# One third-feature block per token block moved from a DMA transpose to TensorE, with the first products reordered around the turns

## The chip, the cores and the metric

The kernel runs on one core of a Trainium2 chip. The metric is the time of one execution in device microseconds. TensorE multiplies matrices, VectorE and ScalarE do elementwise work and read TensorE's results out of PSUM, GpSimd (POOL in the profile) does small elementwise work, and SyncE (SP) issues most DMAs. [...]

## The reference

The input `x` has 2048 tokens (L) of 640 features (H), all in bfloat16. Two branches work on the same `x`, and a gate per token mixes them.

```python
    def _A_ref(x, Lambda_re, Lambda_im, B_re, B_im, C_re, C_im, log_dt, Dskip):
        ...
        Lam_bar = jnp.exp(dt * Lam)
        B_bar = ((Lam_bar - 1.0) / Lam)[:, None] * Bmat
        Bu = jnp.einsum("bld,pd->blp", x + 0j, B_bar)
        ...
        for t in range(L):
            h = Lam_bar[None, :] * h + Bu[:, t, :]
            hs.append(h)
        hseq = jnp.stack(hs, 1)
        y = 2.0 * jnp.einsum("blp,dp->bld", hseq, Cmat).real + x * Dskip[None, None, :]
        return y

    def _B_ref(x, w1, b1, w2, b2):
        h = jnp.einsum("bsd,df->bsf", x, w1) + b1
        h = _gelu(h)
        return jnp.einsum("bsf,fd->bsd", h, w2) + b2

    x = A_x
    g = _sigmoid((x * gate_w).sum(-1, keepdims=True))
    ...
    return g * a + (1 - g) * b
```

Branch A is a diagonal complex state-space model with 640 states; branch B is a two-layer perceptron with 1728 hidden units.

## The kernel before

**Tiles and stages.** Tokens are cut into four chunks of 512 (`CH`), each of four blocks of 128 (`TPC` = 4). Where the change speaks of "tokens 0 and 1" it means token blocks 0 and 1 of the first chunk. Features are cut into five blocks of 128 (`KD` = 5), and the hidden units of branch B into 14 blocks (`KF`). TensorE contracts over partitions, so the products need `x` with features on partitions: `xT[c]` holds chunk c as [feature in block, feature block, token]. `xn[c]` holds the same chunk as it lies in memory, tokens on partitions. The program goes through stages that it writes out at its end: `ff1` (first layer of B), `ssm` (input product of A and its scans), `fin_b` (second layer of B) and `fin_a` (output product of A), for the four chunks in an interleaved order.

**The start, where the change lies.** The first products, L361 to L397, compute the first six hidden blocks (`FA` = 6) of chunk 0. They accumulate in six PSUM banks, `banks[0..5]`, over the five feature blocks. Two ways bring chunk 0's features onto partitions:

- Feature blocks 0 and 1 (`KA` = 2) are loaded plainly into `xn[0]` by `load_x0`, one DMA per token block, and turned by TensorE: `turn` (L239) multiplies a 128 x 128 block of `xn[0]` with the identity into a PSUM bank, and `turned` (L243) copies the result into `xT[0]`, on VectorE for feature block 0 and on ScalarE for feature block 1. `turn_first(a, other, t)` does both for token block a.
- Feature blocks 2, 3 and 4 come by two DMA transposes (`load_turned`, L149), one for token blocks 0 and 1, one for 2 and 3. The plain copy of these features for later use in branch A is loaded much later (L186, L187).

All turns write into two PSUM banks, `pA` and `pT`. `pT` takes feature block 0 and `pA` feature block 1, each with 128 columns per token block. `pA` has another use at L391.

**PSUM.** `bank()` (L75) hands out tiles of one pool, `ps`, of eight buffers[...]. At the start `pA`, `pT` and the six `banks` are alive. The next tile, `pP` (L373), is for turning a small array of parameters, `prmA`; its copy into `colA` (L375) starts a chain on VectorE and ScalarE that makes sine and cosine tables for branch A.

**The first products.** `strip(kd, t0, t1, f0, f1)` issues the products of feature block kd with tokens t0 to t1 for hidden blocks f0 to f1, one matmul each, and `part(kd, a)` is a strip over token block a and all six hidden blocks. Weights for feature block kd and the six hidden blocks are in `w1a[kd]`.

**What sets the order.** For TensorE, VectorE and ScalarE the order in the program is the order on the engine (`manual_schedule`, L195). Each engine runs its own instructions in that order and waits where one needs a result of another. DMAs go out from SP's queue and, for three of the first loads, from ScalarE's, in program order as well: x of token blocks 0, 1 and 3 and `w1a[2]` on SP; `w1a[0]`, `w1a[1]` and x of block 2 on ScalarE; then the two transposes, `w1a[4]`, `w1a[3]`, `w1b`, `w1c` and the weights of branch A on SP. GpSimd's queue loads the small parameters. Later in the program a small clock model (`ck`, with `pend` and `let_out`) decides where VectorE's scan work is placed; it is entered with `ff1_mm` through `pe(cols)`, which only adds columns.

Of the kernel before, what the change touches and what calls it, by code (L numbers as in the profile page):

```python
# [16 lines left out]
P = 128  # L17
T = 2048
D = 640
# [3 lines left out]
KD = D // P  # L23
# [5 lines left out]
H = TPC // 2  # L29
HT = H * P  # L30
KSA = 2
HD = D // 2
FA = 6
# [8 lines left out]
def kernel(  # L42
# [19 lines left out]
    nc = tc.nc  # L62
    x2d = A_x.flatten_outer_dims()
# [11 lines left out]
    def bank(dtype=F32):  # L75
        return ps.tile([P, CH * 4 // (4 if dtype == F32 else 2)], dtype, name="bank")
# [6 lines left out]
    xT = [const.tile([P, KD, CH], BF16, name=f"xT{c}") for c in range(NCH)]  # L83
# [41 lines left out]
    def load_w1a(queue, kd):  # L125
        queue.dma_start(out=w1a[kd][:], in_=B_w1[kd * P:(kd + 1) * P, 0:cut1])
# [2 lines left out]
        queue.dma_start(out=dst, in_=v.rearrange("(j p) -> j p", p=P))  # L129

    KA = 2
    xn[0] = xnp.tile([P, TPC, D], BF16, name="xn")

    def load_x0(queue, a0, a1, d0, d1):
        queue.dma_start(out=xn[0][:, a0:a1, d0:d1], in_=x2d[a0 * P:a1 * P, d0:d1].rearrange("(a p) d -> p a d", p=P))

    load_x0(nc.sync, 0, 1, 0, KA * P)
    load_w1a(nc.scalar, 0)
    load_x0(nc.sync, 1, 2, 0, KA * P)
    load_w1a(nc.scalar, 1)  # L140
    load_x0(nc.sync, 3, 4, 0, KA * P)
    load_x0(nc.scalar, 2, 3, 0, KA * P)
    load_w1a(nc.sync, 2)
# [2 lines left out]
    warm = const.tile([P, 1], F32, name="warm")  # L146
    nc.scalar.activation(out=warm[:], in_=nc.const_aps.tensor(1.0, [P, 1], BF16), func=ACT.Exp)

    def load_turned(a):  # L149
        nc.sync.dma_start_transpose(out=xT[0][:, KA:KD, a * P:(a + H) * P], in_=x2d[a * P:(a + H) * P, KA * P:D])  # L150

    load_turned(0)
    load_turned(H)
    load_w1a(nc.sync, 4)
    load_w1a(nc.sync, 3)
    for kd in range(KD):
# [26 lines left out]
        nc.sync.dma_start(out=w2_sb[:, k0:k1, :], in_=B_w2[k0 * P:k1 * P, :].rearrange("(kf p) d -> p kf d", p=P))  # L183
    for h in range(2):
        nc.sync.dma_start(out=w2l[h * F_LAST:(h + 1) * F_LAST, :], in_=B_w2[(KF - 1) * P:F, :])
    load_x0(nc.sync, 0, H, KA * P, D)  # L186
    load_x0(nc.sync, H, TPC, KA * P, D)  # L187
    nc.sync.dma_start(out=b2bc[:], in_=B_b2.rearrange("(o d) -> o d", o=1).to_broadcast([P, D]))
    nc.sync.dma_start(out=Dbc[:], in_=A_Dskip.rearrange("(o d) -> o d", o=1).to_broadcast([P, D]))
# [45 lines left out]
    pA = bank()  # L235
# [3 lines left out]
    def turn(p, col, a, kd):  # L239
        nc.tensor.matmul(p[:, col:col + P], lhsT=xn[0][:, a, kd * P:(kd + 1) * P], rhs=ident[:], start=True, stop=True,  # L240
                         skip_group_check=True)

    def turned(engine, p, col, a, k0, k1):  # L243
        dst = xT[0][:, k0:k1, a * P:(a + 1) * P]
        src = p[:, col:col + (k1 - k0) * P].rearrange("p (k t) -> p k t", t=P)
        if engine is nc.vector:
            nc.vector.tensor_copy(out=dst, in_=src)
        else:
            nc.scalar.activation(out=dst, in_=src, func=ACT.Identity)

    def turn_first(a, other, t=None):
        t = t or bank()
        turn(t, a * P, a, 0)
        turned(nc.vector, t, a * P, a, 0, 1)
        turn(other, a * P, a, 1)
        turned(nc.scalar, other, a * P, a, 1, 2)

    pT = bank()
# [16 lines left out]
    def ff1_mm(p, c, kf, kd, t0=0, t1=CH, first=None, last=KD - 1):  # L275
        w, f0 = (w1a, 0) if kf < FA else (w1b, FA) if kf < FB else (w1c, FB)
        w = w[kd][:, (kf - f0) * P:(kf - f0 + 1) * P]
        nc.tensor.matmul(p[:, t0:t1], lhsT=w, rhs=xT[c][:, kd, t0:t1],  # L278
                         start=(kd == 0) if first is None else first, stop=(kd == last), skip_group_check=first is not None)
        pe(t1 - t0)  # L280
# [53 lines left out]
    def strip(kd, t0, t1, f0=0, f1=FA):  # L334
        for kf in range(f0, f1):
            ff1_mm(banks[kf], 0, kf, kd, t0, t1, kf not in begun, 3)
            begun.add(kf)
# [17 lines left out]
    def over(c, n):  # L355
        return c.rearrange("p (k o) -> p k o", o=1).to_broadcast([P, KS, n])

    def part(kd, a):
        strip(kd, a * P, (a + 1) * P)

    for _ in range(3):  # L361
        nc.tensor.matmul(banks[0][:, 0:P], lhsT=ones(P), rhs=ones(P), start=True, stop=True, skip_group_check=True)  # L362
    turn_first(1, pA, pT)
    part(0, 0)
    part(0, 1)
    strip(1, 0, HT, 0, FA // 2)
    turn_first(3, pA, pT)
    strip(1, 0, HT, FA // 2, FA)
    turn_first(2, pA, pT)
    part(0, 3)  # L370
    part(1, 3)
    part(0, 2)
    pP = bank()  # L373
    nc.tensor.matmul(pP[:, 0:2 * KS], lhsT=prmA[:], rhs=ident[:, 0:2 * KS], start=True, stop=True, skip_group_check=True)  # L374
    nc.vector.tensor_copy(out=colA[:], in_=pP[:, 0:2 * KS])  # L375
# [1 line left out]
    nc.vector.tensor_scalar(out=limp[:], in0=lim_c, scalar1=INV_2PI, scalar2=None, op0=ALU.mult)  # L377
    nc.vector.tensor_tensor(out=thp_c[:], in0=dt16[:], in1=limp[:], op=ALU.mult)
    nc.vector.tensor_tensor(out=u, in0=tf[:].rearrange("p (o i) -> p o i", o=1).to_broadcast([P, KS, NP]), in1=over(thp_c[:], NP), op=ALU.mult)
    part(1, 2)  # L380
    strip(2, 0, HT)
    nc.vector.tensor_copy(out=kk[:], in_=u)
# [48 lines left out]
    for ks in range(KS):  # L431
        for dst, X, xs, Y in ((TCOS, FS, nsH, FC), (TSIN, FC, sH, FS)):
            t = work.tile([P, HB], F32, name="g")
# [305 lines left out]
```

## Time and profile before

| What | Value |
|---|---|
| Median of 8 runs | 215.14 us (214.58 to 216.46) |
| The profiled execution's own time | 215.41 us |
| Its span | 213.5 us |
| TensorE, VectorE, ScalarE, POOL busy | 98%, 86%, 48%, 29% of the span |
| Products of the first layer from `w1a` (L278) | 152 matmuls, mean 340 ns |
| Turns (L240) | 8 matmuls, from 3.36 to 6.90 us |
| Cast out of a turn on VectorE (L247), on ScalarE (L249) | 0.29 us, 0.28 us |

The span runs from the first to the last instruction that the profiler recorded; the execution's own time also holds what lies around it. In the timeline, each line gives a start in us from the span's start, a duration, the engine, the line of the kernel, what is written and read, and how many instructions were merged; what stands in brackets is the idle time before and what ended it. PE is TensorE's multiplication and PEld its loading of the stationary operand. A duration of a matmul includes its latency, so the distance from start to start tells how long it holds TensorE.

### The profile page before, as it was taken

How to read it: one execution, taken by the hardware profiler on the slowest of the kernel's cores; microseconds unless marked ns; L12 is line 12 of the kernel's file. 1: busy time of each engine (PE TensorE's matmuls, PEld its weight loads, DVE VectorE, ACT ScalarE, POOL GpSimd, SP SyncE). 2: the span in 40 equal slices, each digit the busy share in tenths (PEclk: the TensorE clock that was granted, in tenths of full speed). 3: DMA queues.
4: the chain of work that ended last, by engine and by line, in shares of the span. 5: the costliest groups of instructions: out<-in, count | busy, mean ns of one | idle time of the engine just before them, and what ended most of it. 6: DMA issues, size and time to landing. Idle time of an engine off the chain costs nothing.

```text
span 213.5 us, 3580 instructions
## 1 busy us (share of the span) xinstructions
PE 209.3 (98%) x1365; PEld 125.7 (59%) x1376; DVE 183.2 (86%) x335; ACT 102.1 (48%) x184; POOL 62.8 (29%) x101
## 2 busy tenths in 40 slices
PE   8999999999999999999999999999999999999994
PEld 5844444454576644775457777444457587676773
DVE  1589999999998999999999999999999999903153
ACT  3499856665858588203663210456682422305100
POOL 7035069854441563404145503055000000000000
PEclk9999999999999999999999999999999999999999
DMA  6999999997000000061000005100000000100011
GB/s 185 249 179 216 231 232 341 244 185 186 3 0 0 0 3 0 12 186 64 0 0 3 0 1 186 61 0 0 0 3 15 0 3 31 61 31 3 0 63 64
DMA packets 33314, 16.24 MB, mean 76 GB/s; under 512 B 24720, under 2 KB 33296, under 8 KB 33296
## 3 DMA queue, kind: packets, MB, share of 16 engines
q1 hardware_dynamic: 32560, 15.50, 30.2%
q10 hardware_dynamic: 576, 0.49, 0.7%
q8 instruction: 11, 0.18, 0.3%
q14 instruction: 7, 0.06, 0.1%
q0 software_dynamic: 160, 0.01, 0.1%
HBM read 7.48 MB, written 2.62 MB: 47 GB/s over the span
## 4 chain that ended last, share of the span: by engine, by line
PE 98%; issue 0%; DVE 0%
PE bank L606 27%; PE bank L278 27%; PE bank L665 20%; PE bank L549 20%; PE bank L237 1%; PE bank L622 1%; PE bank L300 1%; PE bank L240 0%; DVE ot L670 0%; PE bank L362 0%; PE bank L391 0%; PE bank L374 0%
## 5 line engine op out<-in xcount | busy, mean ns | idle before, releaser
L606 PE MATMUL bank<-w_sb,gel 128*128 128x384 bf16 (+1 forms) x416 | 57.9, 299 | 0.0
L606 PEld LDWEIGHTS <-gel 128*128 128x128 bf16 x416 | 40.3, 98 | 17.0 <-issue 0.8
L552 ACT ACTIVATE bu<-bank 128x512 bf16<-128x512 f32 x40 | 23.6, 606 | 37.5 <-PE bank L549 37.5
L283 ACT ACTIVATE gel<-bank,colB 128x512 bf16<-128x512 f32 x52 | 34.0, 695 | 10.8 <-PE bank L278 10.6
L665 PEld LDWEIGHTS <-hs 128*128 128x128 bf16 x330 | 31.7, 98 | 11.6
L513 POOL TENSOR_SCALAR e<-g,cq 128x2 f32<-128x2 bf16 x15 | 18.3, 1222 | 64.3 <-DVE g L506 64.3
L506 DVE TENSOR_TENSOR_SCAN g<-r_c,carry,v 128x512 bf16<-128x512 f32 x30 | 37.2, 1270 | 0.0
L614 ACT ACTIVATE gb<-bank,gcol 128x384 f32<-128x384 f32 (+1 forms) x32 | 15.1, 526 | 33.7 <-PE bank L622 16.8
L278 PE MATMUL bank<-xT,w1a 128*128 128x512 bf16 (+2 forms) x152 | 27.9, 340 | 0.2
L665 PE MATMUL bank<-CT_re,hs 128*128 128x320 bf16 (+2 forms) x165 | 27.1, 295 | 0.0
L665 PE MATMUL bank<-CT_im,hs 128*128 128x320 bf16 (+2 forms) x165 | 27.1, 295 | 0.0
L670 DVE SCALAR_TENSOR_TENSOR ot<-bank,gcol,gb 128x320 bf16<-128x320 f32 (+2 forms) x33 | 17.4, 532 | 9.7 <-PE bank L665 9.5
L549 PE MATMUL bank<-xT,BT_im 128*128 128x512 bf16 x99 | 24.8, 379 | 0.1
L549 PE MATMUL bank<-xT,BT_re 128*128 128x512 bf16 x97 | 24.4, 379 | 0.2
L278 PEld LDWEIGHTS <-w1a 128*128 128x128 bf16 x156 | 14.4, 103 | 11.7
L580 DVE TENSOR_TENSOR bank<-xn,Dbc 128x320 f32<-128x320 bf16 (+2 forms) x33 | 14.5, 483 | 7.0 <-ACT gb L614 7.0
L278 PE MATMUL bank<-xT,w1b 128*128 128x512 bf16 x80 | 17.9, 379 | 0.0
L549 PEld LDWEIGHTS <-BT_im 128*128 128x128 bf16 x100 | 9.8, 98 | 11.8
L549 PEld LDWEIGHTS <-BT_re 128*128 128x128 bf16 x100 | 9.6, 98 | 11.0
L515 POOL TENSOR_TENSOR carry<-e,e 128x1 f32<-128x1 f32 x30 | 15.8, 547 | 1.2
L487 DVE TENSOR_TENSOR v<-wa,wb 128x512 bf16<-128x512 bf16 x40 | 15.2, 422 | 0.6
L595 ACT ACTIVATE bank<-b2bc 128x384 f32<-128x384 bf16 (+1 forms) x24 | 11.7, 529 | 7.1 <-DVE ot L670 7.1
(110 smaller groups left out, 216.6 us busy)
## 6 DMA issues: line engine op xcount, KB each, us to landing
out_dram<-ot SPq DMA_DIRECT2D x15, 160.0 KB, 1.8
w_sb<-in_B_w_dram SPq DMA_DIRECT2D x2, 640.0 KB, 6.0
xn<-in_A_x_dram SPq DMA_DIRECT2D x2, 640.0 KB, 4.2
w_sb<-in_B_w_dram SPq DMA_DIRECT2D x1, 800.0 KB, 9.6
w1b<-in_B_w_dram SPq DMA_DIRECT2D x5, 128.0 KB, 3.3
xn<-in_A_x_dram SPq DMA_DIRECT2D x4, 160.0 KB, 2.8
w1a<-in_B_w_dram SPq DMA_DIRECT2D x3, 192.0 KB, 3.4
w1a<-in_B_w_dram ACTq DMA_DIRECT2D x2, 192.0 KB, 3.0
```

What stands on the lines that cost most here:

```text
L278: nc.tensor.matmul(p[:, t0:t1], lhsT=w, rhs=xT[c][:, kd, t0:t1], start=(kd == 0) if first is None else first, stop=(kd == last), skip_grou ...
L283: nc.scalar.activation(out=gel[c][:, kf, :], in_=p[:, :], func=ACT.Gelu_apprx_tanh, bias=b1_c[:, kf:kf + 1])
L487: nc.vector.tensor_tensor(out=o, in0=a, in1=b, op=op)
L506: nc.vector.tensor_tensor_scan(s["g"][:, ri, :], r_c[:, ks:ks + 1].to_broadcast([P, CH]), s["v"][:, ri, :], init, ALU.mult, ALU.add)
L513: nc.gpsimd.tensor_scalar(out=t[:], in0=g[:, :, CH - 1], scalar1=f[:, ks:ks + 1], scalar2=None, op0=ALU.mult)
L515: nc.gpsimd.tensor_tensor(out=carry[:, ri, ks:ks + 1], in0=m[0][:, ri:ri + 1], in1=m[1][:, 1 - ri:2 - ri], op=op)
L549: nc.tensor.matmul(p[:], lhsT=BT[ks >= KSA][:, kd, (ks % KSA if ks < KSA else ks - KSA) * P:][:, 0:P], rhs=xT[c][:, kd, :], start=(kd == 0 ...
L552: nc.scalar.activation(out=bu[:, ri, :], in_=p[:], func=ACT.Identity)
L606: nc.tensor.matmul(p[:, col:col + d1 - d0], lhsT=gel[c][:, kf, a * P:(a + 1) * P], rhs=w2_sb[:, kf, d0:d1], start=False, stop=False, skip_ ...
L614: nc.scalar.activation(out=gbs[ti][:, d0:d1], in_=p[:, col:col + d1 - d0], func=ACT.Identity, scale=gcol[:, 1, ti:ti + 1])
L665: nc.tensor.matmul(p[:, 0:d1 - d0], lhsT=hs[c][:, j, lo:lo + P], rhs=CT[:, j % KS, d0:d1], start=False, stop=(j == 2 * KS - 1), skip_group ...
L670: nc.vector.scalar_tensor_tensor(out=ot[:, d0:d1], in0=p[:, 0:d1 - d0], scalar=gcol[:, 0, ti:ti + 1], in1=gbs[ti][:, d0:d1], op0=ALU.mult, ...
```

## The change

Token blocks 0 and 1 now load three feature blocks plainly (`KB` = 3), and the first DMA transpose brings only feature blocks 3 and 4 for them. The second transpose still brings three. The late plain load of the rest of token blocks 0 and 1 becomes one feature block narrower. TensorE makes two more turns, for feature block 2 of token blocks 0 and 1; the first goes into `pT` with its copy on VectorE, the second into `pA` with its copy on ScalarE. They stand ahead of `pP`.

The products of feature blocks 0 and 1 are issued in another order. Three of the six products of token block 0 go ahead of the turn of token block 1. Block 3 is turned earlier, and the products of feature block 1 with token blocks 0 and 1 become two parts of 128 columns in place of two half strips of 256 columns. `part(0, 2)` and `part(1, 2)` stand after `pP`'s matmul and the instructions of VectorE and ScalarE that follow it in the program.

```diff
     KA = 2
+    KB = 3
...
-    load_x0(nc.sync, 0, 1, 0, KA * P)
+    load_x0(nc.sync, 0, 1, 0, KB * P)
     load_w1a(nc.scalar, 0)
-    load_x0(nc.sync, 1, 2, 0, KA * P)
+    load_x0(nc.sync, 1, 2, 0, KB * P)
...
-    def load_turned(a):
-        nc.sync.dma_start_transpose(out=xT[0][:, KA:KD, a * P:(a + H) * P], in_=x2d[a * P:(a + H) * P, KA * P:D])
-
-    load_turned(0)
-    load_turned(H)
+    def load_turned(a, k):
+        nc.sync.dma_start_transpose(out=xT[0][:, k:KD, a * P:(a + H) * P], in_=x2d[a * P:(a + H) * P, k * P:D])
+
+    load_turned(0, KB)
+    load_turned(H, KA)
...
-    load_x0(nc.sync, 0, H, KA * P, D)
+    load_x0(nc.sync, 0, H, KB * P, D)
...
+    strip(0, 0, P, 0, FA // 2)
     turn_first(1, pA, pT)
-    part(0, 0)
+    strip(0, 0, P, FA // 2, FA)
+    part(1, 0)
+    turn_first(3, pA, pT)
     part(0, 1)
-    strip(1, 0, HT, 0, FA // 2)
-    turn_first(3, pA, pT)
-    strip(1, 0, HT, FA // 2, FA)
+    part(1, 1)
+    part(0, 3)
     turn_first(2, pA, pT)
-    part(0, 3)
     part(1, 3)
-    part(0, 2)
+    for a, t, engine in ((0, pT, nc.vector), (1, pA, nc.scalar)):
+        turn(t, a * P, a, KA)
+        turned(engine, t, a * P, a, KA, KB)
     pP = bank()
     nc.tensor.matmul(pP[:, 0:2 * KS], lhsT=prmA[:], rhs=ident[:, 0:2 * KS], start=True, stop=True, skip_group_check=True)
...
+    part(0, 2)
     part(1, 2)
     strip(2, 0, HT)
```

## The prediction

> **What bounds the kernel now.** I read the page first: busy times, then the chain that ended last. TensorE is busy for 98% of the span and the chain is TensorE from end to end.
>
> ```profile
> span 213.5 us, 3580 instructions
> PE 209.3 (98%) x1365; PEld 125.7 (59%) x1376; DVE 183.2 (86%) x335; ACT 102.1 (48%) x184; POOL 62.8 (29%) x101
> ...
> PE 98%; issue 0%; DVE 0%
> ```
>
> The view of waits, cut to TensorE, has one row for the whole execution: the start itself.
>
> ```profile
> PE bank L237 <- PEq L723: 0.8, 1, 0.8
> ```
>
> So nothing that makes data arrive sooner shortens this execution; time is won or lost only by what TensorE must issue, by gaps between its instructions, and by its clock. Busy time cannot show short gaps, because the ends of matmuls are modelled and overlap the next start. The timeline's start times show them. I read it around the turns (L240), which the change multiplies.
>
> ```profile
> 3.68 0.29 DVE L247 CAST xT<-bank 128x128 bf16<-128x128 f32 x1 [2.21 <-PE bank L240]
> ...
> 4.03 0.37 PE L240 MATMUL bank<-ident,xn 128*128 128x128 bf16 x2
> ...
> 6.81 0.31 PE L240 MATMUL bank<-ident,xn 128*128 128x128 bf16 x2
> ...
> 6.95 1.17 PE L278 MATMUL bank<-xT,w1a 128*128 128x128 bf16 x18
> 7.06 0.29 DVE L247 CAST xT<-bank 128x128 bf16<-128x128 f32 x1 [0.31 <-PE bank L240]
> 7.15 0.28 ACT L249 ACTIVATE xT<-bank 128x128 bf16<-128x128 f32 x1 [0.30 <-PE bank L240]
> 7.90 0.10 PEld L374 LDWEIGHTS <-prmA 128*128 128x128 bf16 x1
> 7.96 0.17 PE L374 MATMUL bank<-ident,prmA 128*128 128x10 bf16 x1
> ```
>
> Three readings. (a) Slot: 18 products of 128 columns between 6.95 and 7.96 are 0.056 us each. Before about 6.5 us the starts stand twice as far apart (4.20, 4.30, 4.41, 4.52): 0.107 us. (b) Token block 1's turn starts at 4.03, just after the cast out of block 0's part of the same bank ended (3.68 + 0.29 = 3.97), although it writes other columns. At 6.46 + 0.29 = 6.75 the cast of block 3 ended, and block 2's turn follows at 6.81. So a turn waits for the last copy out of its bank. (c) That round trip, turn to copy to next use of the bank, is 0.25 (6.81 to 7.06) + 0.29 + 0.06 = 0.60 us by VectorE, and 0.25 + 0.28 + 0.05 = 0.58 us by ScalarE.
>
> Of the DMA transposes I read issue and landing:
>
> ```profile
> L150 SPq DMA_TRANSPOSE xT<-in_A_x_dram x2: 1275/1300/1325, 2.6 to 4.0; - x2
> ...
> DMA to landing us min/median/max: 3.8/4.2/4.6
> ```
>
> The first is issued at 2.59 and lands 4.6 later, at 7.2; the second at 3.97 + 3.8 = 7.8. The groups by window put their first users, the products of 256 columns, at 8.3 (blocks 0 and 1) and 9.0 (blocks 2 and 3): 1.1 and 1.2 us of slack.
>
> [...] 0.107 us a slot, then 0.056, with the switch near 6.5 us. [...] The first x load (64 KB, issued on SP) and w1a_0 (192 KB, on ACT), both issued at 0.72, land 2.6 and 2.8 us later[...].
>
> **The change, part by part.**
>
> *Bigger x loads.* Blocks 0 and 1 bring 96 KB each instead of 64; the number of DMA issues on SP and ACT stays. Upper bound: 32 KB at the page's 185 GB/s for the first slice is 0.18 us. Lower: w1a_0 carries 128 KB more than the x load and lands 0.2 us later, so 0.05 for 32 KB. I take 0.1 us later for the first turn (3.36). TensorE is then on the half clock[...]: **+0.05** (0.02 to 0.18). Block 1's load, landing about 0.2 to 0.3 late near 4.0, is covered: its turn now follows the first three products, near 4.45. w1a_0 and w1a_1, up to 0.2 late, are used near 4.13 and 5.0, against landings at 3.5 and 4.3.
>
> *Shorter transpose.* Six blocks of 128 x 128 become four, so SP's issue falls from 1.33 to about 0.88 us and the other transpose, w1a_4, w1a_3, w1b and w1c go out about 0.4 us earlier. TensorE waits for none: **0**.
>
> *Two more turns.* 2 x 0.056 = **+0.11**. One more 0.29 us cast and one 0.28 us activation lie on engines that idle there (0.84 and 0.96 us before L375 and L376).
>
> *The order.* The products are the same in number of columns; six of 256 columns become twelve of 128, equal within 0.02. Three products ahead of block 1's turn need only w1a_0 and block 0's first cast, for which the turn itself waited before: 0. Block 3's turn comes nine products after block 1's: covered. Then two short covers:
>
> 1. Block 2's turn, six products (block 1 of features, token block 3), then block 0's third-feature turn into `pT`. Starts would be 8 slots apart, 0.45 us; the bank needs 0.60: **+0.15**. The turn into `pA` needs 0.58 after block 2's, which has passed by then.
> 2. `pP = bank()` is the ninth tile of a pool of eight. `pA` and six accumulators live on, so it can only take `pT`'s bank. Before, 18 products stood between the last turn and pP's matmul (6.81 to 7.96, against 0.60 needed). Now pP follows the last `pT` turn after one turn: 0.11 against 0.60, **+0.49**. In TensorE's queue behind it stand part(0, 2), part(1, 2) and everything later. They do not need pP, but cannot pass.
>
> The old order has a smaller case, which goes: at 6.81 and 6.90 block 2's turns started together about 0.06 later than the spacing allows: **-0.06**.
>
> Bounds for the two covers: 0.35 if the copies answer 0.15 faster each, 0.9 if a wait costs 0.13 more each. Nothing below zero: an instruction cannot precede the copy it waits for.
>
> *Who waits for pP.* The colA copy on VectorE and the chain behind it, sine tables included. By the sum pP goes from 7.96 to about 8.35, 0.4 later, whereas TensorE's products after it go 0.74 later. GELU and table work therefore gain cover, and no later wait is made. POOL's queue is not touched except for colA's reader at 8.45, which no one awaits soon.
>
> Sum: 0.05 + 0.11 + 0.15 + 0.49 - 0.06 = **+0.74 us**. As TensorE never waits later, nothing gives it back. The profiled execution, 215.41 us, becomes 216.15. It lies 0.27 above the median of 215.14, inside the scatter of 214.58 to 216.46; taken to the median: **215.9 us**, +0.34%, own range 215.5 to 216.4. A measurement of this kernel tells some 0.3%, 0.65 us, from no change.
>
> **Rivals.**
>
> *The bank wait is mostly covered (0.15).* If the copies are back sooner or pP gets another bank, only the start and the turns remain: +0.16, 215.3. Against it: readings (b) and (c), and the count of the banks.
>
> [...]
>
> *The data is what binds elsewhere, and the change is faster (0.15).* Place: the products of feature block 2, L381. With the clock up at 4.2 instead of 6.5 they would start (6.5 - 4.2)/2 = 1.15 earlier, at 7.15, just where the first transpose lands. In executions without the profiler it may land later still; the change takes blocks 0 and 1 off that transpose. Decision point: the wait removed must exceed 0.74, and 1.4 for a gain that can be told, so a landing 1.4 us after the need. That gives 214.4 or less. Against: 1.1 us of slack and no DMA wait on TensorE.
>
> **How the numbers follow.** My forecast holds 0.62, of which 0.08 falls inside 0.65 us since its centre stands near that line. Slower: 0.54 + 0.08[...] = 0.62. Same: 0.08 + 0.15 = 0.23. Faster: 0.15. The range 214.4 to 217.0 takes in the bounds of the covers, the mostly covered rival and the near part of the faster one; about 0.1 is left below and 0.07 above.
>
> **What would show it.** In the timeline after: ten turns; block 0's third-feature turn about 0.60 after block 2's; pP's matmul about 0.60 after that, with TensorE starting nothing between but one turn; the first product of feature block 2 near 9.0 instead of 8.3; the spacing of later products unchanged. Wrong if pP's matmul follows the turn within 0.2 us, if products of L278 wait for a DMA[...].

## The result: slower by a quarter of a per cent, and the profile after

| | Median | Runs |
|---|---|---|
| Before | 214.71 us (214.28 to 216.46) | 58 |
| Changed | 215.22 us (214.86 to 216.06) | 21 |

The ratio is 1.0026 with a 95% interval of 1.0015 to 1.0036: +0.56 us, from 0.32 to 0.77 (the two medians differ by 0.51). The change costs time, as forecast. The centre is below the 0.74 us of the forecast and below the 0.3% that I had called the least that can be told; the interval still reaches to 0.77, so this number by itself does not contradict the size.

The page of the changed kernel still has TensorE as its chain. A cast on VectorE (L248) has entered it.

```profile
span 213.1 us, 3597 instructions
...
PE 208.6 (98%) x1373; PEld 125.1 (59%) x1384; DVE 183.6 (86%) x336; ACT 102.7 (48%) x185; POOL 63.1 (30%) x101
...
PE 98%; DVE 0%; issue 0%
PE bank L611 27%; PE bank L279 26%; PE bank L670 20%; PE bank L554 20%; PE bank L238 1%; PE bank L627 1%; PE bank L301 1%; PE bank L241 0%; DVE xT L248 0%; DVE ot L675 0%; PE bank L378 0%; PE bank L396 0%
```

The span is 0.4 us *shorter* than before, although the kernel is slower: the profiled execution, 214.93 us, had an early clock. Its products are one slot of 0.056 us apart from the first one at 3.97; in the profile of before that spacing began near 6.5, after 0.107 us. By full clock and half rate I mean these two spacings alone: the granted clock reads 1.00 in the profile of before at both, from 4.20 to 6.30 and from 7.00 to 7.90. The 2.5 us between 4.0 and 6.5 at half rate are worth some 1.25 us (an estimate from the two slots: half of them). Two single executions of this kernel can't be compared by their spans.

What can be compared is the distance between starts. The view of waits, cut to TensorE's products and then to its weight loads, has two new rows that name another engine or a DMA:

```profile
PE bank L378 <- DVE xT L248: 0.3, 1, 0.3
```

```profile
PEld L241 <- DMA xn<-in_A_x_dram: 0.2, 1, 0.2
```

And the timeline of the changed kernel around the last turns, with start and duration in front:

```profile
6.07 0.28 PE L241 MATMUL bank<-ident,xn 128*128 128x128 bf16 x2
...
6.18 0.50 PE L279 MATMUL bank<-xT,w1a 128*128 128x128 bf16 x6
6.33 0.29 DVE L248 CAST xT<-bank 128x128 bf16<-128x128 f32 x1 [0.82 <-PE bank L241]
...
6.67 0.27 PE L241 MATMUL bank<-ident,xn 128*128 128x128 bf16 x2
...
6.93 0.29 DVE L248 CAST xT<-bank 128x128 bf16<-128x128 f32 x1 [0.31 <-PE bank L241]
...
7.27 0.17 PE L378 MATMUL bank<-ident,prmA 128*128 128x10 bf16 x1 [0.33 <-DVE xT L248]
```

The six products from 6.18 end their slots at 6.52; the third-feature turn starts at 6.67, 0.60 after block 2's turn at 6.07. That is the hole of 0.15. `pP`'s product starts at 7.27, again 0.60 after the turn, where two turns fill only 0.11: the hole of 0.49. The brackets show 0.33 for it, and the first hole has no bracket at all, since the modelled end of a product covers its first part. Both holes stand where the forecast put them.

### The profile page after: what moved, and what is told of

Read it like the earlier page. It is cut to its first block, busy times and chain, and to the rows that moved or that the text cites. A ratio compares the mean times of both kernels' runs of the same rounds, so it can differ in the third digit from the quotient of the medians.

```text
span 213.1 us, 3597 instructions
## 1 busy us (share of the span) xinstructions
PE 208.6 (98%) x1373; PEld 125.1 (59%) x1384; DVE 183.6 (86%) x336; ACT 102.7 (48%) x185; POOL 63.1 (30%) x101
## 4 chain that ended last, share of the span: by engine, by line
PE 98%; DVE 0%; issue 0%
PE bank L611 27%; PE bank L279 26%; PE bank L670 20%; PE bank L554 20%; PE bank L238 1%; PE bank L627 1%; PE bank L301 1%; PE bank L241 0%; DVE xT L248 0%; DVE ot L675 0%; PE bank L378 0%; PE bank L396 0%
## 5 line engine op out<-in xcount | busy, mean ns | idle before, releaser
L279 PE MATMUL bank<-xT,w1a 128*128 128x512 bf16 (+2 forms) x158 | 27.0, 322 | 0.3
L279 PEld LDWEIGHTS <-w1a 128*128 128x128 bf16 x162 | 13.9, 98 | 12.2 <-issue 0.6
```

## The experiments

Ten kernels gave results, two of them twice. Times without a gate scatter by over 1 us, and in the ungated traces the slot of TensorE falls from 0.107 to 0.056 us (the clock rises, as I call it) at moments from 3.7 to 6.6 us. So most kernels were gated: a wait ahead of the first turn is to make the executions start the real work at one time, at full clock, with the first inputs landed.

```diff
     pA = bank()
-    for n in (512, 512, 512, 512, 512, 128, 128, 128, 128):
-        nc.tensor.matmul(pA[:, 0:n], lhsT=ones(P), rhs=ones(n), start=True, stop=True)
+    gate = work.tile([P, 2, CH], BF16, name="v")
+    nc.vector.memset(gate[:], 0.0)
+    for _ in range(5):
+        nc.scalar.activation(out=gate[:], in_=gate[:], func=ACT.Identity)
+    for _ in range(22):
+        nc.tensor.matmul(pA[:, 0:512], lhsT=ones(P), rhs=ones(512), start=True, stop=True)
+    nc.tensor.matmul(pA[:, 0:512], lhsT=ones(P), rhs=gate[:, 0, :], start=True, stop=True)
```

The first turn then starts at 9.20 in the traces, with slots of 0.056 us in those of g_before_2 and g_after, and most runs of one kernel agree within 0.15 us. Six of the 41 gated executions are 1.2 to 1.6 us longer, with a mean granted clock of 0.992 where the others have 0.998 or more; one of them is the profiled execution of g_before, in which TensorE had waited 1.9 us at the gate (0.9 to 1.7 in the other traces) and ran at half rate from 10.45 to 13.7. The table compares traces of the others.

| Gated kernel | Median, us | Last five output products start at | Against before |
|---|---|---|---|
| before, second set | 220.19 | 215.05 | |
| changed | 220.56 | 215.50 | +0.45 |
| changed, pP late | 220.39 | 215.33 | +0.28 |
| changed, part(0, 2) and part(1, 2) as covers | 220.53 | 215.48 | +0.43 |
| before, new order alone | 219.85 | 214.75 | -0.30 |
| changed, all covers, pP in pT's bank | 220.09 | 214.96 | -0.09 |
| before, pP early | 220.59 | 215.53 | +0.48 |

The third column is the last row of TensorE's timeline. I compare by it, since it leaves out what lies after the last product and outside the span. The first set ran on another chip: g_before, and with it the changed kernel, pP late and the covers. Medians compared within each set say much the same: +0.46, +0.29 and +0.43 for these three against 220.10, and -0.34, -0.10 and +0.40 for the last three rows against 220.19. So differences below 0.1 us rest on the traces.

**g_before and g_before_2: the kernel before, gated.**

> The kernel before with a gate ahead of its first turn: 22 dummy products keep TensorE busy while ScalarE writes a scratch tile five times, and one last dummy product waits for that tile. TensorE then starts its real work near 9.1 us in every execution, at full clock and with all first inputs landed. Both theories expect the same of it, some 218 to 220 us, no DMA wait at the turns, and a spread of its runs below the 2.2 us of the kernel before. It is the base of the other gated kernels. In its trace block 2's turn should stand about 0.15 us later than the slots allow, because block 3's turn is only 8 slots ahead (0.45 us against a 0.60 us round trip of the bank).

> The gated kernel before again, as the base of this set, expected at 220.1 us as in the set before. Its trace at full clock should show two holes of about 0.15 us on TensorE that the half clock of the ungated profile hid: ahead of part(0, 1), whose first product needs the cast of block 1's turn 8 slots (0.45 us) after it, and ahead of block 2's turn. And next to none ahead of the last hidden tile (L300), where ScalarE's chain from pP through the sine tables and the GELUs ends about when TensorE arrives.

The first set had a median of 220.10, the second 220.19 us. The timeline of the second shows one of the two holes:

```profile
11.05 0.27 PE L245 MATMUL bank<-ident,xn 128*128 128x128 bf16 x2
...
11.16 0.49 PE L283 MATMUL bank<-xT,w1a 128*128 128x256 bf16 x3
11.31 0.29 DVE L252 CAST xT<-bank 128x128 bf16<-128x128 f32 x1 [0.97 <-PE bank L245]
...
11.65 0.27 PE L245 MATMUL bank<-ident,xn 128*128 128x128 bf16 x2
```

Three products of 256 columns from 11.16 take 0.33; the turn comes at 11.65, not at 11.49: 0.16. A narrower window shows the other, inside one row:

```profile
10.19 0.43 PE L283 MATMUL bank<-xT,w1a 128*128 128x128 bf16 x2
```

The sixth product of part(0, 0) starts at 10.19 and the next at 10.39, 0.21 later where a slot is 0.056, hence 0.15. It waits for the cast of block 1, turned at 9.80. So at full clock the old order has 0.31 us of the same holes. At half rate eight slots of 0.107 last 0.86 us, longer than the round trip of 0.67 measured there, and the holes are gone: in the profile that I forecast from, the first was hidden and the second nearly so. The trace of g_before, whose clock had fallen to half rate there, shows the same program without the second hole:

```profile
11.84 0.84 PE L283 MATMUL bank<-xT,w1a 128*128 128x256 bf16 x3
12.48 0.42 PE L245 MATMUL bank<-ident,xn 128*128 128x128 bf16 x2
```

Here the three products take 0.64 us, and block 2's turn follows at once. Back in the trace at full clock, L305 (L300 ungated) starts at 24.61, one slot after the product before it, while ScalarE's bias for its bank had ended just before, at 24.53:

```profile
24.07 0.46 ACT L298 ACTIVATE bank<-b1x 128x260 f32<-128x260 bf16 x1
...
24.61 0.26 PE L305 MATMUL bank<-w1c_lo,xT 128*128 128x65 bf16 x3
```

ScalarE's chain has next to no slack there.

**g_after: the changed kernel, gated.**

> The changed kernel with the same gate. Theory (waits for PSUM banks on TensorE): slower than the gated kernel before by 0.11 for two turns, 0.15 and 0.49 for the two short covers, less 0.15 for the short cover of the kernel before, so +0.60 us. Rival (the loss comes from later x data and the changed order of DMAs): with all inputs landed before the first turn the loss goes, leaving the two turns, +0.11 us.

+0.45. The rival, +0.11, falls: with the first inputs landed, most of the loss stays.

```profile
11.69 0.28 PE L246 MATMUL bank<-ident,xn 128*128 128x128 bf16 x2
11.80 0.50 PE L284 MATMUL bank<-xT,w1a 128*128 128x128 bf16 x6
12.29 0.27 PE L246 MATMUL bank<-ident,xn 128*128 128x128 bf16 x2
12.89 0.17 PE L383 MATMUL bank<-ident,prmA 128*128 128x10 bf16 x1 [0.33 <-DVE xT L253]
```

Its holes are 0.15 (11.80 with six products, turn at 12.29) and 0.49 (turn 12.29, pP 12.89). From the traces: 0.11 for the turns + 0.15 + 0.49 - 0.15 - 0.16 = 0.44. The 0.15 between this and the +0.60 expected is the hole at part(0, 1), which I had not counted when I wrote it.

**g_pP_late: pP behind the products that it held up.**

```diff
+    part(0, 2)
+    part(1, 2)
     pP = bank()
     nc.tensor.matmul(pP[:, 0:2 * KS], lhsT=prmA[:], ...)
...
-    part(0, 2)
-    part(1, 2)
     strip(2, 0, HT)
```

> The gated changed kernel with pP moved behind part(0, 2) and part(1, 2), so 12 products stand between the last turns and pP's matmul. Theory: the 0.49 us hole ahead of pP goes and the 0.15 us one ahead of the third-feature turn stays, so +0.11 us against the gated kernel before and -0.49 against the gated changed one. Rival (data): the same as the gated changed kernel.

-0.17 against the changed kernel, not -0.49. The hole ahead of pP is gone, but another has opened ten microseconds later, ahead of the last hidden tile:

```profile
24.13 0.59 PE L284 MATMUL bank<-xT,w1c_hi 128*128 128x512 bf16 x2
24.36 0.47 ACT L299 ACTIVATE bank<-b1x 128x260 f32<-128x260 bf16 x1
...
24.88 0.27 PE L306 MATMUL bank<-w1c_lo,xT 128*128 128x65 bf16 x3 [0.16 <-ACT bank L299]
```

Two products of 512 columns from 24.13 take 0.43, so L306 could start at 24.56; it starts at 24.88, 0.32 later, when ScalarE has written the bank. ScalarE gets to that instruction in order, after the copies, the sines and the GELUs, and all of those stand behind colA, hence behind pP. pP stands six products later in TensorE's order than before, six products are 0.33 us, and the wait is 0.32. The link shows in five of the seven gated traces at full clock: ScalarE's instruction starts 11.27 to 11.30 us after pP's product, wherever pP stands (11.40 in g_share, 11.47 in g_b_pP_early). So pP's place is a trade: early, TensorE waits for the bank; late, it waits for ScalarE.

**g_covers: more products in front of each wait.**

```diff
+    part(0, 2)
     for a, t, engine in ((0, pT, nc.vector), (1, pA, nc.scalar)):
         turn(t, a * P, a, KA)
         turned(engine, t, a * P, a, KA, KB)
+    part(1, 2)
     pP = bank()
...
-    part(0, 2)
-    part(1, 2)
     strip(2, 0, HT)
```

> The gated changed kernel with part(0, 2) ahead of the third-feature turns and part(1, 2) between them and pP. Theory: first cover 14 slots (0.78 us against 0.60) closes its hole; second cover 8 slots, 0.45 against 0.60, leaves 0.15 ahead of pP. So again +0.11 us against the gated kernel before. With pP_late it tells whether each hole is a matter of slots alone. Rival (data): the same as the gated changed kernel.

+0.43: my expectation was wrong by two waits. The first hole did not close, it moved: part(0, 2) needs block 2's cast itself, and waits 0.15 for it. The second shrank to 0.15 as expected. But pP is late, and L306 waits 0.28. The rival's figure is met here by another cause, as these three holes in the trace show.

**g_b_pP_early: the main suspect by itself.**

```diff
     turn_first(2, pA, pT)
+    pP = bank()
+    nc.tensor.matmul(pP[:, 0:2 * KS], lhsT=prmA[:], ...)
     part(0, 3)
     part(1, 3)
     part(0, 2)
-    pP = bank()
-    nc.tensor.matmul(pP[:, 0:2 * KS], lhsT=prmA[:], ...)
```

> The gated kernel before with one thing of the change: pP's matmul straight after the last turns, with nothing between. Theory: a hole of 0.49 us on TensorE ahead of pP. pP is now 18 products ahead of its old place, so ScalarE's chain has slack and nothing is given back: +0.49 us, some 220.6 us. Rival (an earlier pP relieves ScalarE's chain and returns part of it): +0.2 us or less.

+0.48. Nothing is given back.

```profile
11.64 0.27 PE L245 MATMUL bank<-ident,xn 128*128 128x128 bf16 x2
...
11.90 0.29 DVE L252 CAST xT<-bank 128x128 bf16<-128x128 f32 x1 [0.31 <-PE bank L245]
...
12.24 0.17 PE L376 MATMUL bank<-ident,prmA 128*128 128x10 bf16 x1 [0.33 <-DVE xT L252]
```

From 11.64 to 12.24 is the 0.60 us round trip, of which two turns fill 0.11.

**g_b_order, b_order and b_order_3: the new order without the rest.**

```diff
-    turn_first(1, pA, pT)
-    part(0, 0)
-    part(0, 1)
-    strip(1, 0, HT, 0, FA // 2)
-    turn_first(3, pA, pT)
-    strip(1, 0, HT, FA // 2, FA)
+    strip(0, 0, P, 0, FA // 2)
+    turn_first(1, pA, pT)
+    strip(0, 0, P, FA // 2, FA)
+    part(1, 0)
+    turn_first(3, pA, pT)
+    part(0, 1)
+    part(1, 1)
     turn_first(2, pA, pT)
     part(0, 3)
     part(1, 3)
     part(0, 2)
```

> The gated kernel before with the new order of the first products alone: no third-feature turns, no wider loads, transposes as before, block 2's turn ahead of part(0, 3) so that every cover is 11 slots or more. Theory (bank waits in both kernels): both 0.15 us holes of the kernel before go, -0.30 us against the gated kernel before, some 219.80 us. Rival (the kernel before has no holes to lose, the order is worth nothing): 220.1.

-0.30, with neither hole in the trace. This order is not quite that of the changed kernel, which turns block 2 after part(0, 3). Not gated (b_order_2, the same kernel, gave no time):

> The kernel before, not gated, with the new order of the first products alone (loads, transposes and turns as before). Theory: the gain is the holes that the old order has, which depend on when the clock rises: 0.30 us when it is up before the first turns, some 0.06 when it rises near 6.5 us as in the profile of before. So -0.05 to -0.30 us, some 214.6 against 214.8, a ratio of 0.9987 to 0.9998 that may not clear its interval. Rival (order is worth nothing, or the DMAs then bind): 1.000 or above, with a DMA wait on TensorE after block 0's cast in the trace.

> The new order alone on the kernel before, not gated, once more, since its first set left -0.21 to +0.34 us. Theory: it saves the two holes of the old order whenever the clock is up early enough, so -0.05 to -0.30 us, a ratio of 0.9986 to 0.9998. Rival (what the order saves is waited for again at a DMA or at ScalarE's chain): a ratio of 1.000 or above.

1.0003 (0.9990 to 1.0016) and 0.9999 (0.9990 to 1.0007): no difference that can be told. A gain of over 0.21 us is outside both intervals, a smaller one is not. The two traces have clocks that rise near 5.4 and 6.5 us and no hole of this kind. With a clock that rises near 6.5 the old order had 0.06 to lose; for one near 5.4 I estimate one of its two holes, since block 2's turn and the products ahead of it then run at full clock. So what the order is worth on average ungated stays open.

**g_share and a_share: the changed kernel with its holes closed.** The order is that of g_b_order; then:

```diff
     part(1, 3)
-    for a, t, engine in ((0, pT, nc.vector), (1, pA, nc.scalar)):
+    part(0, 2)
+    for a, t in ((0, pT), (1, pA)):
         turn(t, a * P, a, KA)
-        turned(engine, t, a * P, a, KA, KB)
-    pP = bank()
+    pP = pT[:, 3 * P:4 * P]
     nc.tensor.matmul(pP[:, 0:2 * KS], lhsT=prmA[:], ...)
     nc.vector.tensor_copy(out=colA[:], in_=pP[:, 0:2 * KS])
+    for a, t, engine in ((0, pT, nc.vector), (1, pA, nc.scalar)):
+        turned(engine, t, a * P, a, KA, KB)
...
-    part(0, 2)
     part(1, 2)
-    strip(2, 0, HT)
+    strip(2, HT, CH)
...
-    strip(2, HT, CH)
+    strip(2, 0, HT)
```

> The gated changed kernel with all covers: order as in g_b_order, then the two third-feature turns, then pP's product into a corner of pT's bank next to them, with no copy between, colA copied first, and feature block 2 of token blocks 2 and 3 ahead of that of blocks 0 and 1. Theory: only the two turns remain on top of g_b_order, +0.11 us, some 219.9 us; no hole ahead of pP. Rival (the two turns themselves, or their copies, cost more than their slots): over 220.1.

-0.09 against before, +0.21 against g_b_order: 0.11 for two turns and 0.09 of wait at L306. No hole is left around pP: its product starts at 12.59, one slot after the turn at 12.53, although that turn has just written the same bank.

> The changed kernel, not gated, with all covers and pP in a corner of pT's bank, as in g_share. Theory: against the changed kernel it loses the 0.15 and 0.49 us holes and gains 0.09 ahead of the last hidden tile; against the kernel before it keeps two turns and, with an early clock, 0.19 us of wait for block 1's x: -0.1 to +0.2 us. So no difference that can be told from the kernel before. Rival (the wide loads and shorter transpose are what costs): as slow as the changed kernel, +0.5 us.

Ungated it is 1.0015 (1.0006 to 1.0024), +0.32 us (0.13 to 0.52): slower than the kernel before, and, from separate sets, some 0.2 below the changed one. The expectation was too low, and the rival's +0.5 lies at the edge of the interval, so the ungated times do not decide between them. This order asks for the second transpose earlier, and in the trace its first product of 256 columns waits for it:

```profile
8.13 0.92 PE L279 MATMUL bank<-xT,w1a 128*128 128x256 bf16 x7 [0.16 <-DMA xT<-in_A_x_dram]
```

The last product of 128 columns starts at 7.75, so by the distance of starts the hole is 0.33 us. That is about what the expectation lacks, in this one execution.

**b_wide_loads: the bigger loads alone.**

```diff
-    load_x0(nc.sync, 0, 1, 0, KA * P)
+    load_x0(nc.sync, 0, 1, 0, 3 * P)
...
-    load_x0(nc.sync, 1, 2, 0, KA * P)
+    load_x0(nc.sync, 1, 2, 0, 3 * P)
...
-    load_x0(nc.sync, 0, H, KA * P, D)
+    load_x0(nc.sync, 0, H, 3 * P, D)
```

> The kernel before, not gated, with only the 96 KB loads of x for token blocks 0 and 1 in place of 64 KB; transposes stay at three feature blocks, so 64 KB more are moved early. Theory: the first turn hardly moves (0 to 0.1 us), block 1's x lands near 4.3 instead of 3.7 and its turn, which follows block 0's at once in the old order, waits some 0.25 us for it[...]. So +0.1 to +0.3 us. Rival (the loads are free): no change and no DMA wait at the turns.

1.0010 (1.0001 to 1.0020), +0.21 us. The turns wait for x, and a place is hit that I had left out: the products of feature block 2, waiting for the first transpose. First the waits of the weight loads, then the timeline:

```profile
PEld L240 <- DMA xn<-in_A_x_dram: 0.5, 2, 0.3
```

```profile
4.21 0.29 PE L240 MATMUL bank<-ident,xn 128*128 128x128 bf16 x2
...
7.22 0.49 PE L278 MATMUL bank<-xT,w1a 128*128 128x128 bf16 x6
8.12 0.92 PE L278 MATMUL bank<-xT,w1a 128*128 128x256 bf16 x7 [0.40 <-DMA xT<-in_A_x_dram]
```

Six slots from 7.22 end at 7.55, and the next product starts at 8.12: 0.57. The clock was up by 4.3 us, and the first transpose landed 5.5 us after its issue, where it took 4.6 in the profile of before. The loads of this kernel were wide, so the trace does not say how long the kernel before waits here.

This is also the old order at an early clock and without a gate, and both of its holes are in the trace. Part(0, 1) starts 0.21 us after the product at 4.61, and the other hole is this:

```profile
5.59 0.49 PE L278 MATMUL bank<-xT,w1a 128*128 128x256 bf16 x3
6.08 0.27 PE L240 MATMUL bank<-ident,xn 128*128 128x128 bf16 x2
```

They are 0.15 and 0.16 us, as in the gated kernel.

## Why the prediction was right in its cause and off in its size

**The two short covers (+0.15, +0.49): right.** 0.15 and 0.49 in the changed kernel, gated and not, and +0.48 when pP's place alone is changed. The round trip of 0.60 us, read off the profile of before, held in the traces at full clock; at half rate it was 0.67 there, from the turn at 3.36 to the next at 4.03.

**Two turns (+0.11): right** as far as g_share shows, +0.21 with 0.09 of wait elsewhere.

**The old order's own holes (-0.06): the step that failed.** At full clock they are 0.31, by the gated kernel before, by the -0.30 of g_b_order, and, ungated, in the trace of b_wide_loads. I took the 0.06 from one execution whose clock rose at 6.5, in the middle of these instructions. I did consider an early clock, but only for the rival in which the data binds elsewhere, and did not ask what it does to this term. A cast out of a bank took 0.29 us at either clock in the profile of before (at 3.68 and at 7.06), while the slots that cover it halved, from 0.107 to 0.056. The gated sum is 0.44 where mine would be 0.69 without the start. It is not shown that this term is what makes +0.56 of +0.74 ungated: the interval holds both, the new order alone gained nothing there that can be told, and the next term errs the other way. With two errors of opposite sign, part of the nearness of 0.56 to 0.74 is luck.

**Bigger loads (+0.05): too small, and partly in the wrong place.** That half of a 0.1 us delay would count, since the turn is at half rate, was my estimate, from slots of 0.107 and 0.056; it supposes that a later turn does not put off the rise of the clock, which was not shown. The first turn hardly moved (3.28 after, 3.36 before). Block 1's load, which I had called covered, landed at 4.28, 3.1 us after its issue, and its turn waited 0.2 because the clock was early; in the trace of a_share, with the clock still at half rate, the load landed 2.8 us after its issue and the same turn did not wait. Alone, on the old order, the loads cost 0.21 (0.02 to 0.43). The ungated loss of 0.56 is 0.1 above the gated 0.45, which is the size of such waits, but the interval is too wide to show that they are the difference.

**Shorter transpose (0): right in effect, wrong on the queue.** SP's issue did not fall to 0.88 us:

```profile
L151 SPq DMA_TRANSPOSE xT<-in_A_x_dram x2: 1272/1290/1307, 2.6 to 3.9; - x2
...
DMA to landing us min/median/max: 3.4/3.9/4.3
```

1.31 us for four blocks after 1.33 for six, and 1.27 for the second transpose, which still has six, so w1a_4 goes out at 5.26, as before at 5.29. The first transpose landed 4.3 us after its issue, where it was 4.6; but six blocks took 4.4 and 4.7 in the traces of the new order, and four took 5.1 in that of a_share, so a gain in landing is not shown.

**Who waits for pP: right, and closer to the edge than I said.** No wait was made at L301 in the changed kernel, since pP stands earlier in the order. g_pP_late shows that the kernel before is at the limit there.

**The rivals.** *Mostly covered* fell: 0.49 is in the trace. *Half rate lasting longer after the change*, the 0.08 that I gave to slower beside my forecast, was an estimate and was not seen: in six ungated profiled executions the spacing fell to one slot between 3.7 and 6.6 us, in the changed kernel by its first product at 3.97, against 6.5 in the profile of before. What sets the moment was not shown. *The data binds elsewhere*: such a hole exists, 0.57 us in the trace of b_wide_loads at an early clock and with its later landing (5.5 us after the issue), and my 1.1 us of slack was that of a late clock. It did not make the change faster. How often the kernel before waits so was not tried; no trace of it with an early clock was taken ungated.

**The sum**: the sign, the place and the main terms held; +0.74 was +0.56, at 0.26% inside the 0.3% that I had given to no change. Hole by hole the sum is shown for the gated kernels. How the +0.56 divides between holes and data ungated stays open: with its holes closed the changed kernel still loses 0.32.

## What to carry to other kernels

A wait for a copy on another engine hardly changed with TensorE's clock here (0.60 us at full, 0.67 at half rate), while the cover, counted in products, lasted half as long at full clock (0.056 a slot, not 0.107). So work out the cover at full clock as well as at the clock of the profile at hand. In this full pool a new tile took the bank of the tile just released, and its first writer waited for that tile's last copy (a hole of 0.49 us in the changed kernel), with all that stood behind it; writing into a corner of a bank that TensorE had just written avoided it (0.06 us from turn to product in g_share). A gate (first turn at 9.20 us in the traces, a granted clock of 0.998 or more in 35 of 41 executions) turned differences of 0.1 us, lost in a scatter of over 1 us, into sums that can be checked hole by hole.

## What the runs showed of the hardware that I had not expected

- A DMA transpose of 256 tokens by two feature blocks held SP's queue for 1.31 us, two of three feature blocks for 1.33 and 1.27.
- At full clock a PSUM bank went from a 128-column product over a copy on VectorE back to TensorE in 0.60 us, the same in the first profile and in the gated ones.
- The idle time in brackets and the view of waits understate short holes of TensorE: 0.33 for 0.49, 0.16 for 0.33, and nothing for 0.15. The distance of starts, less the slots issued, gives them.
